# Attention and a feed-forward layer on one core: the two score groups of a head pair computed together, and a written order of the feed-forward products around them

## The chip, the core and the metric

One core of a Trainium2 chip. The metric is the device time of one execution in microseconds (us); lower is better. The core has TensorE (PE; its weight loads are listed as PEld), VectorE (DVE), ScalarE (ACT), GpSimd (POOL) and SyncE (SP), which issues nearly all transfers. Each engine works its own queue in order; semaphores join them.

## What is computed

Attention over 8 batches x 8 heads, head size 64, 512 local and 32 global tokens. A global query attends to all 544 keys; a local query to the 32 global keys and to the local keys within 32 positions. Then a feed-forward layer over the 4608 tokens:

```python
s_ll = np.where(np.abs(pos[:, None] - pos[None, :]) <= 32, scale * q_l @ k_l.T, -1e9)
out_l = sm(concat(scale * q_l @ k_g.T, s_ll)) @ concat(v_g, v_l)
out_g = sm(scale * q_g @ concat(k_g, k_l).T) @ concat(v_g, v_l)
x = attention output as (4608, 512)
h = x @ w_in                                   # 512 -> 2048
g = maximum(h, 0) + log1p(exp(-abs(h)))
out = g @ w_out                                # 2048 -> 512
```

Everything is in fp32. The feed-forward splits each operand in a high and a low part and forms three products (high x high, low x high, high x low).

## The kernel before

**Feed-forward** (`moe_items`). The tokens are worked in blocks: eight of 512 local tokens, b = 0 to 7 (one batch each), and one of 256 global tokens. A block has 16 tiles f of the hidden layer. The product H f (`hpart`) is 12 matmuls of 128x512 into one PSUM bank of the pool `ps_h` (tag `h`, two banks, used in turn). `act` follows: Abs, Exp and Ln on ACT, `e` on DVE (it reads the bank a last time), the high part `gh` on ACT, the low part `gl` on POOL. The product O f (`opart`, in two halves of two token tiles) is 12 matmuls from `gh`, `gl` and `w_out` into four banks that hold the block's output until O 15; then the results are copied out (`ot`, two on DVE and two on ACT). O f stands two H tiles behind H f. Before H 0 of a block, `split_x` makes `xh` (ACT) and `xl` (DVE) of the block's four inputs `xa`, one for each head pair of the batch.

**Attention.** The 32 head pairs m are four to a batch. Pairs 0 to 5 are worked ahead of the feed-forward, pairs 6 to 31 in pieces between its products. The pieces of a pair:
- `scores(m, 0)` and `scores(m, 1)`: each is 512 columns for both heads (chunks of 160, 192, 160 and of 32, 192, 192, 96), fp32, with 64 rows of the array to a head; into a two-bank tile of `ps_a` (tag `a`, one buffer, shared with the values). From pair 8 on DVE adds the mask while it reads the banks (L318) and takes the maxima of blocks (L319). Each group is followed by transfers of the next pair's queries and keys (`load`).
- `maxima` and `probs`: POOL and DVE fold the maxima (L331 to L344), DVE spreads them (L352), POOL subtracts (L355, five instructions), ACT takes the exponential (L357, one for each group), DVE sums blocks (L361).
- `totals`: the sums are folded and inverted (L331 to L372, result `rb`).
- `values` and `normalise`: 12 matmuls into the tile `a` (1024 columns for each head: chunks of 160, four times 192, and 96), then five DVE instructions (L392 to L397) that write `xa`.

The matmuls of scores and values are plain fp32, and each shows twice in the trace: 12 and 16 records for the two score groups, 24 for the values.

**Order.** Every piece has a slot number: 12 for each pair, plus 0 and 6 for the scores, 17 (`TOT`) for the totals and 21 (`VAL`) for the values. The feed-forward items are emitted in turn; after each, all pieces with a slot up to `at` are emitted, where `at` grows by 48 over a block. So a block holds four pairs, and the two score groups and the values of a pair stand at three places. The weights are split on ACT, DVE and POOL (L466 to L484) during block 0. A scheduling layer then places the instructions in the queues.

Of the kernel before, what the change touches and what calls it, by code (L numbers as in the profile page):

```python
# [8 lines left out]
F32 = mybir.dt.float32  # L9
# [4 lines left out]
ALU = mybir.AluOpType  # L14
# [5 lines left out]
P = 128  # L20
# [3 lines left out]
NPC = 3  # L24
# [8 lines left out]
MPE = 8  # L33
VAL = 21
TOT = 17
STEP = 3
GW = 75
W_AHEAD = 13
W_PRE = 16
START = 79  # L40
RATE = 3
# [15 lines left out]
def moe_over_global_local_attention(  # L57
# [235 lines left out]
    def scores(m, g):  # L293
        if "o" not in banks:
            ps = ps_s.tile([P, 2, 512], F32, tag=("oA", "oB")[g], name=f"s_ps{m}_{g}")
        else:
            ps = ps_a.tile([P, 2, 512], F32, tag="a", name=f"s_ps{m}_{g}")
        pe_mask = m < MPE
        cut = slice(512 * g, 512 * g + 512)
        for h in range(2 if pe_mask else 0):  # L300
            mm(ps[:, h], lhsT=ident, rhs=mask[:, cut], start=True, stop=False, skip_group_check=True)
        for c, o, qs, w in CHUNKS:
            if not cut.start <= o < cut.stop:
                continue
            raw, ks, o = st["raw", m, c // 2], QW[c // 2] + 128 * (c % 2), o - cut.start
            for h in range(2):
                r = slice(64 * h, 64 * h + 64)
                mm(ps[:, h, o:o + w], lhsT=raw[r, ks:ks + P], rhs=raw[r, qs:qs + w],
                   start=not pe_mask, stop=True, skip_group_check=True)
# [5 lines left out]
        if pe_mask:  # L315
            nc.scalar.copy(s, ps)  # L316
        else:
            nc.vector.tensor_tensor(s, ps, mask[:, cut].unsqueeze(1).to_broadcast([P, 2, 512]), op=ALU.add)  # L318
        order["scores"] = nc.vector.tensor_reduce(windows(st["mt", m], 4 + 16 * g, 36, 2, 16), s.rearrange("p h (b k) -> p h b k", k=32),  # L319
                                axis=AX.X, op=ALU.max, apply_transpose=True).ins  # L320

    def grid(t, start, *dims):
# [78 lines left out]
    def pieces():  # L401
        def piece(*fs):
            def go():
                for f in fs:
                    f()
            return go
        ps = []
        for m in range(M0, M):
            for g in range(2):
                fs = [lambda m=m, g=g: scores(m, g)]  # L410
                if m + 1 < M:
                    fs += [lambda m=m, p=p: load(m + 1, p) for p in ((0,), (1, 2))[g]]
                ps.append((12 * m + 6 * g, piece(*fs)))
                if g:
                    fs = [lambda m=m: maxima(m)] + [lambda m=m, q=q: probs(m, q) for q in range(2)]
                    ps.append((12 * m + (6 if m > M0 else 9), piece(*fs)))
            ps.append((12 * m + TOT, lambda m=m: totals(m)))
            fs = [lambda m=m: values(m), lambda m=m: normalise(m)]
            if m + 2 < M:
                fs.append(lambda m=m: load_v(m + 2))  # L420
            ps.append((12 * m + VAL, piece(*fs)))
        ps.sort(key=lambda t: t[0])
        return ps
# [74 lines left out]
    def moe_items():  # L498
# [119 lines left out]
    loads(W_PRE + 1)  # L618
    first = 12 * (H // 2 - 1) + VAL + STEP
    pcs = pieces()  # L620
# [12 lines left out]
    for k in range(-2, n + 2):  # L633
        stage(k + 2, 0)

        while k >= n - 2 and pcs[0][0] < min(12 * M0 + 4 * (k - n + 3), START):
            pcs.pop(0)[1]()
# [98 lines left out]
```

## Time and profile before

| | us |
|---|---|
| median of 3 runs (997.62 to 998.42) | 998.16 |
| the profiled execution | 998.89 |
| its span, first to last instruction | 997.0 |
| PE busy | 961.7 (96%), 5236 matmul records |
| PEld busy | 764.6 (77%) |
| DVE / ACT / POOL busy | 630.2 / 512.2 / 435.1 |

The profiled execution lies 1.9 us above its span, and 0.7 us above the median. On the page's chain that ended last PE holds 77%, of which the H and O products are 34% and 32% of the span, the scores 4% and the values 4%. A matmul's end is modelled and matmuls overlap in the records, so the distance from start to start tells more than the busy time.

### The profile page before, as it was taken

Reading aid. Unit: us, or ns where it says so; the run is one execution under the profiler, and the core shown is the slowest. Engines: PE = TensorE matmul, PEld = TensorE weight load, DVE = VectorE, ACT = ScalarE, POOL = GpSimd, SP = SyncE. Lnnn points to the kernel's source line nnn. Section 1 sums busy time; section 2 is a strip of 40 time slices with the busy share of each in tenths; the row PEclk is TensorE's granted clock in tenths of the full one; section 3 lists DMA queues with packets and bytes.
Section 4 is the critical chain, followed back from the end, with each engine's and each line's share of the span. In section 5 each row is a group of like instructions: output and inputs, shape, how many; then the busy total and the mean of one; then the engine's idle time right before and its main releaser. Section 6 shows DMA issues by size and latency. Waiting matters only on the chain.

```text
span 997.0 us, 14310 instructions
## 1 busy us (share of the span) xinstructions
PE 961.7 (96%) x5236; PEld 764.6 (77%) x5239; DVE 630.2 (63%) x1272; ACT 512.2 (51%) x890; POOL 435.1 (44%) x580
## 2 busy tenths in 40 slices
PE   6798999989999999999999999999999999999998
PEld 4576777767777777777787777777787788888896
DVE  6888959666668766776668666776677665311211
ACT  5785655644445544444455444454455445544553
POOL 5655756534444544443444444444434444222221
PEclk9897999989999999999999999999999999999999
DMA  9824231121112211121112111221112100200010
GB/s 363 304 76 160 96 99 35 59 74 40 37 49 70 70 49 39 47 91 33 49 50 80 39 49 49 70 70 38 48 48 75 49 17 2 65 1 1 1 43 22
DMA packets 34326, 66.20 MB, mean 66 GB/s; under 512 B 7632, under 2 KB 11472, under 8 KB 34256
## 3 DMA queue, kind: packets, MB, share of 16 engines
q1 hardware_dynamic: 33440, 65.19, 19.9%
q8 instruction: 41, 0.67, 0.3%
q14 instruction: 29, 0.24, 0.1%
q10 hardware_dynamic: 816, 0.10, 0.1%
HBM read 55.84 MB, written 9.44 MB: 65 GB/s over the span
## 4 chain that ended last, share of the span: by engine, by line
PE 77%; DVE 10%; POOL 5%; ACT 4%; issue 3%; POOLq 0%; ACTq 0%; DVEq 0%
PE h L124 34%; PE o L124 32%; PE s_ps L124 4%; PE v_ps L124 4%; POOL s L355 2%; POOL gl L533 1%; ACT e L171 1%; DVE mt L319 1%; DVE xl L439 1%; DVE wbitswi L475 1%; PE o0g L124 1%; DVE wiraw L478 1%; DVE woraw L478 1%; DVE sums L168 1%; DVE s L318 1%
## 5 line engine op out<-in xcount | busy, mean ns | idle before, releaser
L124 PE MATMUL h<-xh,wi 128*128 128x512 f32 (+1 forms) x1152 | 348.4, 386 | 6.0 <-DVE e L529 5.9
L124 PE MATMUL o<-wo,gh 128*128 128x512 f32 x1088 | 350.0, 403 | 3.0 <-ACT gh L532 3.0
L533 POOL TENSOR_TENSOR gl<-e,gh 128x512 fp32r<-128x512 f32 x136 | 180.3, 1326 | 314.1 <-ACT gh L532 281.9
L124 PEld LDWEIGHTS h<-xh,wi 128*128 128x128 f32 x1152 | 214.6, 191 | 54.1 <-DVE e L529 9.0
L529 DVE SCALAR_TENSOR_TENSOR e<-h,e 128x512 f32<-128x512 f32 x136 | 93.1, 685 | 248.1 <-ACT e L528 240.6
L124 PEld LDWEIGHTS o<-wo,gh 128*128 128x128 f32 x1088 | 199.0, 189 | 53.6 <-ACT gh L532 3.2
L124 PE MATMUL h<-xl,wi 128*128 128x512 f32 (+1 forms) x576 | 221.1, 384 | 0.0
L124 PE MATMUL o<-wo,gl 128*128 128x512 f32 x544 | 215.6, 396 | 2.3 <-POOL gl L533 2.3
L526 ACT ACTIVATE e<-h 128x512 f32<-128x512 f32 x136 | 81.0, 596 | 220.9 <-PE h L124 220.8
L355 POOL TENSOR_TENSOR s<-s,mb 128x320 f32<-128x320 f32 (+4 forms) x130 | 137.4, 1094 | 68.1 <-DVE mb L352 68.1
L532 ACT CAST gh<-e 128x512 fp32r<-128x512 f32 x136 | 84.5, 622 | 131.1 <-DVE e L529 131.1
L124 PEld LDWEIGHTS h<-xl,wi 128*128 128x128 f32 x576 | 109.7, 190 | 22.8
L124 PEld LDWEIGHTS o<-wo,gl 128*128 128x128 f32 x544 | 102.6, 189 | 29.3 <-POOL gl L533 5.5
L528 ACT ACTIVATE e<-e,one 128x512 f32<-128x512 f32 x136 | 98.8, 726 | 4.3
L527 ACT ACTIVATE e<-e 128x512 f32<-128x512 f32 x136 | 86.1, 633 | 3.8
L361 DVE TRANSPOSE_TENSOR_REDUCE zt<-s 128x32 f32<-128x1024 f32 x52 | 64.5, 1241 | 36.9 <-ACT s L357 36.9
L357 ACT ACTIVATE s<-s 128x1024 f32<-128x1024 f32 x52 | 55.1, 1059 | 31.9 <-POOL mt L312 28.4
L124 PEld LDWEIGHTS s_ps<-raw 64*128 64x128 f32 x728 | 53.9, 186 | 19.1 <-issue 19.1
L319 DVE TRANSPOSE_TENSOR_REDUCE mt<-s 128x32 f32<-128x1024 f32 x52 | 64.1, 1233 | 3.3 <-ACT s L316 2.7
L124 PE MATMUL s_ps<-raw 64*128 64x192 f32 (+3 forms) x728 | 64.4, 313 | 0.3
L318 DVE TENSOR_TENSOR s<-s_ps,mask 128x1024 f32<-128x1024 f32 x48 | 57.7, 1201 | 4.9 <-PE s_ps L124 4.9
L352 DVE STREAM_TRANSPOSE mb<-mt 128x512 f32<-128x512 f32 (+1 forms) x104 | 52.6, 565 | 0.8
(130 smaller groups left out, 826.0 us busy)
## 6 DMA issues: line engine op xcount, KB each, us to landing
raw<-in_qk SPq DMA_DIRECT2D x52, 272.0 KB, 2.7
v<-in_v SPq DMA_DIRECT2D x26, 384.0 KB, 3.1
out<-ot SPq DMA_DIRECT2D x34, 256.0 KB, 2.0
wiraw<-in_w_in SPq DMA_DIRECT2D x16, 512.0 KB, 9.0
woraw<-in_w_out SPq DMA_DIRECT2D x16, 512.0 KB, 8.5
raw<-in_qk SPq DMA_DIRECT2D x26, 224.0 KB, 2.8
v<-in_v SPq DMA_DIRECT2D x6, 512.0 KB, 6.1
raw<-in_qk SPq DMA_DIRECT2D x6, 416.0 KB, 7.9
```

Source lines behind the costliest of these rows:

```text
L124: order["pe"] = after(nc.tensor.matmul(*a, **k), "pe").ins
L318: nc.vector.tensor_tensor(s, ps, mask[:, cut].unsqueeze(1).to_broadcast([P, 2, 512]), op=ALU.add)
L319: order["scores"] = nc.vector.tensor_reduce(windows(st["mt", m], 4 + 16 * g, 36, 2, 16), s.rearrange("p h (b k) -> p h b k", k=32), axis=A ...
L355: nc.gpsimd.tensor_tensor(s[:, :, o:o + w], s[:, :, o:o + w], mb[:, :, q:q + w], op=ALU.subtract)
L357: nc.scalar.activation(s, s, AF.Exp, scale=0.125)
L361: nc.vector.tensor_reduce(windows(st["zt", m], 4 + 16 * g, 36, 2, 16), s.rearrange("p h (b k) -> p h b k", k=32), axis=AX.X, op=ALU.add, a ...
L526: nc.scalar.activation(e, ph, AF.Abs)
L527: nc.scalar.activation(e, e, AF.Exp, scale=-1.0)
L528: nc.scalar.activation(e, e, AF.Ln, bias=one)
L529: nc.vector.scalar_tensor_tensor(e, ph, 0.0, e, op0=ALU.max, op1=ALU.add)
L532: nc.scalar.copy(gh, e)
L533: nc.gpsimd.tensor_tensor(gl, e, gh.bitcast(F32), op=ALU.subtract)
```

## The change

Four things change.

1. From pair 9 on (`WIDE`) the two score groups are emitted together by `both_scores`. The first keeps the tile `a`; the second goes into two single banks of `ps_h`, those of the H products. DVE adds the mask of the second group in two instructions of 512 columns (one to a bank) in place of one of 1024. The three transfers of the next pair are emitted behind both groups, then the block maxima of both.
2. In blocks 1 to 6 the products follow the written list `ORDER`: H is a whole H tile, O a whole O tile, G the next pair's two score groups. Blocks 0, 7 and the global one keep their form.
3. The slots of pairs 6, 7 and 8 are written out (`SLOTS`); from pair 9 on maxima stand at 12 m + 5, totals at + 14, values at + 17.5. The start of block 1 is at slot 55.5 + 48 in place of 60 + 48.
4. Ahead of block 0, `START` is 76 in place of 79, and the slot grows by 3 a step in place of 4.

The core of the diff:

```diff
-VAL = 21
-TOT = 17
-STEP = 3
+VAL = 17.5
+TOT = 14
+WIDE = 9
+FIRST = 55.5
+SLOTS = {6: (72, 75, 78, 86, 90), 7: (81, 87, 87, 97.5, 101.5), 8: (92, 98, 98, 109, 113.5)}
+ORDER = "H O H H O G O H O H H O H O G O H O H H O H O G O H O H H O H H O G O O".split()
-START = 79
+START = 76
...
+        elif m >= WIDE and g:
+            ps = [ps_h.tile([P, 512], F32, tag="h", name=f"s_ps{m}_{g}_{h}") for h in range(2)]
         else:
             ps = ps_a.tile([P, 2, 512], F32, tag="a", name=f"s_ps{m}_{g}")
+        half = (lambda h: ps[h]) if isinstance(ps, list) else (lambda h: ps[:, h])
...
+        elif isinstance(ps, list):
+            for h in range(2):
+                nc.vector.tensor_tensor(s[:, h], ps[h], mask[:, cut], op=ALU.add)
...
+        if m < WIDE:
+            block_maxima(m, g)
...
+    def both_scores(m):
+        scores(m, 0)
+        scores(m, 1)
+        if m + 1 < M:
+            for p in range(NPC):
+                load(m + 1, p)
+        block_maxima(m, 0)
+        block_maxima(m, 1)
...
+            if 0 < b < B - 1:
+                if f == 0:
+                    h = iter(range(NF))
+                    for what in ORDER:
+                        if what == "H":
+                            f = next(h)
+                            items.append((b, 2, 0, lambda b=b, f=f: hpart(b, f, (0, 1))))
+                            items.append((b, 2, 0, lambda b=b, f=f: (hpart(b, f, (2, 3)), act(b, f))))
+                        elif what == "O":
+                            second(done, b)
+                            second(done + 1, b)
+                            done += 2
+                        else:
+                            m = next(wide, None)
+                            if m:
+                                items.append((b, 0, 0, lambda m=m: both_scores(m)))
+                continue
...
-        while k >= n - 2 and pcs[0][0] < min(12 * M0 + 4 * (k - n + 3), START):
+        while k >= n - 2 and pcs[0][0] < min(12 * M0 + 3 * (k - n + 3), START):
```

(`block_maxima` is the instruction of L319, moved into a function.) A block of the list reads, with the numbers of its tiles (O 15 of the block before stands behind H 0): H0 O15 H1 H2 O0 G O1 H3 O2 H4 H5 O3 H6 O4 G O5 H7 O6 H8 H9 O7 H10 O8 G O9 H11 O10 H12 H13 O11 H14 H15 O12 G O13 O14. The values of a pair are emitted behind H 3, H 7 and H 11 and behind O 13. Block 6 has only three G.

**Place 1: PE at the scores.** In the rows, `s_ps_0` is the first group, `s_ps_1` the second, `raw` the queries and keys, `o_0` the first output tile of an O product, `h` an H product. Before, inside block 3 (between the two pieces stand an O, an H, an O and an H product):

```order
L124 MATMUL h_12_4614<-xl_3_3926,wi_1463 128x512
L124 MATMUL s_ps_0_4636<-raw_0_4417 128x160 [waits DMAHW5_49,DVE_49,PE_49]
L124 MATMUL s_ps_0_4636<-raw_0_4417 128x160
L124 MATMUL s_ps_0_4636<-raw_0_4417 128x192 x2
L124 MATMUL s_ps_0_4636<-raw_1_4513 128x160 [waits DMAHW6_49]
L124 MATMUL s_ps_0_4636<-raw_1_4513 128x160
L124 MATMUL o_0_4079<-wo_1488,gh_10_4498 128x512 [waits Activation_49]
...
L124 MATMUL s_ps_1_4733<-raw_1_4513 128x32 [waits PE_49]
L124 MATMUL s_ps_1_4733<-raw_1_4513 128x32
L124 MATMUL s_ps_1_4733<-raw_1_4513 128x192 x2
```

After, at the last G of block 2:

```order
L127 MATMUL o_3_3078<-wo_1607,gl_12_3695 128x512
L127 MATMUL s_ps_0_3803<-raw_0_3571 128x160 [waits DMAHW5_49,PE_49]
L127 MATMUL s_ps_0_3803<-raw_0_3571 128x160
L127 MATMUL s_ps_0_3803<-raw_0_3571 128x192 x2
L127 MATMUL s_ps_0_3803<-raw_1_3573 128x160 [waits DMAHW6_49]
L127 MATMUL s_ps_0_3803<-raw_1_3573 128x160
L127 MATMUL s_ps_1_0_3814<-raw_1_3573 128x32 [waits DVE_49]
L127 MATMUL s_ps_1_1_3815<-raw_1_3573 128x32 [waits DVE_49]
L127 MATMUL s_ps_1_0_3814<-raw_1_3573 128x192
L127 MATMUL s_ps_1_1_3815<-raw_1_3573 128x192
L127 MATMUL s_ps_1_0_3814<-raw_2_3575 128x192 [waits DMAHW7_49]
L127 MATMUL s_ps_1_1_3815<-raw_2_3575 128x192
```

The second group follows the first with no product between, alternates between two tiles, and waits at its first two matmuls for DVE, which is the last reader of those banks.

**Place 2: ACT at the end of a block.** Here `e_14` and `e_15` are the last two tiles of block 3, `xh` the high parts of the next block's inputs. Before:

```order
L526 ACTIVATE e_14_4724<-h_14_4696 128x512 [waits PE_49,Pool_49]
L527 ACTIVATE e_14_4724<-e_14_4724 128x512 [waits Activation_49]
L528 ACTIVATE e_14_4724<-e_14_4724,one 128x512 [waits Activation_49]
L532 CAST gh_14_4729<-e_14_4724 128x512 [waits DVE_49]
L438 CAST xh_0_4871<-xa_0_4130 128x128 [waits PE_49]
L438 CAST xh_0_4871<-xa_0_4130 128x384
L438 CAST xh_1_4877<-xa_1_4361 128x128 [waits PE_49]
L438 CAST xh_1_4877<-xa_1_4361 128x384
L438 CAST xh_2_4883<-xa_2_4592 128x128 [waits PE_49]
L438 CAST xh_2_4883<-xa_2_4592 128x384
L526 ACTIVATE e_15_4801<-h_15_4788 128x512 [waits PE_49,Pool_49]
```

After:

```order
L548 ACTIVATE e_14_4717<-h_14_4704 128x512 [waits PE_49,Pool_49]
L460 CAST xh_0_4881<-xa_0_4160 128x128 [waits PE_49]
L460 CAST xh_0_4881<-xa_0_4160 128x384
L549 ACTIVATE e_14_4717<-e_14_4717 128x512 [waits Activation_49]
L460 CAST xh_1_4887<-xa_1_4393 128x128 [waits PE_49]
L460 CAST xh_1_4887<-xa_1_4393 128x384
L460 CAST xh_2_4893<-xa_2_4626 128x128 [waits PE_49]
L550 ACTIVATE e_14_4717<-e_14_4717,one 128x512 [waits Activation_49]
L460 CAST xh_2_4893<-xa_2_4626 128x384
L548 ACTIVATE e_15_4754<-h_15_4726 128x512 [waits PE_49,Pool_49]
L554 CAST gh_14_4722<-e_14_4717 128x512 [waits DVE_49]
L549 ACTIVATE e_15_4754<-e_15_4754 128x512 [waits Activation_49]
```

The six conversions of `xh` stood behind the work on tile 14; now they stand inside it, and the work on tile 15 begins behind them with `gh_14` between its first and second step.

**Place 3: ACT at the end of block 0.** `wbitswo` and `wo` belong to the last weight tile, `s_1638` to the scores of pair 8. Before:

```order
L532 CAST gh_14_1875<-e_14_1870 128x512 [waits DVE_49]
L357 ACTIVATE s_1638<-s_1638 128x2x512 [waits Pool_49]
L466 ACTIVATE wbitswo_1879<-woraw_1709 128x512 [waits DMAHW2_49]
L438 CAST xh_0_1983<-xa_0_902 128x512 [waits PE_49]
L438 CAST xh_1_1987<-xa_1_999 128x512 [waits PE_49]
L438 CAST xh_2_1991<-xa_2_1548 128x128 [waits PE_49]
L438 CAST xh_2_1991<-xa_2_1548 128x384
L357 ACTIVATE s_1638<-s_1638 128x2x512 [waits Pool_49]
L438 CAST xh_3_1997<-xa_3_1913 128x128 [waits DVE_49,PE_49]
L438 CAST xh_3_1997<-xa_3_1913 128x384 [waits DVE_49]
L526 ACTIVATE e_15_1936<-h_15_1923 128x512 [waits PE_49]
```

After:

```order
L460 CAST xh_0_1969<-xa_0_902 128x512 [waits PE_49]
L554 CAST gh_14_1875<-e_14_1870 128x512 [waits DVE_49]
L460 CAST xh_1_1973<-xa_1_999 128x512 [waits PE_49]
L380 ACTIVATE s_1638<-s_1638 128x2x512 [waits Pool_49]
L488 ACTIVATE wbitswo_1879<-woraw_1709 128x512 [waits DMAHW2_49]
L460 CAST xh_2_1977<-xa_2_1560 128x128 [waits PE_49]
L460 CAST xh_2_1977<-xa_2_1560 128x384
L548 ACTIVATE e_15_1913<-h_15_1900 128x512 [waits PE_49]
L380 ACTIVATE s_1638<-s_1638 128x2x512 [waits Pool_49]
L549 ACTIVATE e_15_1913<-e_15_1913 128x512 [waits Activation_49]
L460 CAST xh_3_1983<-xa_3_1935 128x128 [waits DVE_49]
L550 ACTIVATE e_15_1913<-e_15_1913,one 128x512 [waits Activation_49]
```

Here `xh_0` moves ahead of `gh_14`, `e_15` moves ahead of the second exponential, and the two conversions of `xh_3` end up among the steps of `e_15`. On PE the values of pair 7 stand behind H 15 in place of O 12, and the scores of pair 9 leave this place.

More of the change, by code (lines that the diff above doesn't have):

```diff
@@ L300, in scores @@
         for h in range(2 if pe_mask else 0):
-            mm(ps[:, h], lhsT=ident, rhs=mask[:, cut], start=True, stop=False, skip_group_check=True)
+            mm(half(h), lhsT=ident, rhs=mask[:, cut], start=True, stop=False, skip_group_check=True)
         for c, o, qs, w in CHUNKS:
@@ L307, in scores @@
                 r = slice(64 * h, 64 * h + 64)
-                mm(ps[:, h, o:o + w], lhsT=raw[r, ks:ks + P], rhs=raw[r, qs:qs + w],
+                mm(half(h)[:, o:o + w], lhsT=raw[r, ks:ks + P], rhs=raw[r, qs:qs + w],
                    start=not pe_mask, stop=True, skip_group_check=True)
@@ L316, in scores, with block_maxima @@
             nc.scalar.copy(s, ps)
+        elif isinstance(ps, list):
+            for h in range(2):
+                nc.vector.tensor_tensor(s[:, h], ps[h], mask[:, cut], op=ALU.add)
         else:
             nc.vector.tensor_tensor(s, ps, mask[:, cut].unsqueeze(1).to_broadcast([P, 2, 512]), op=ALU.add)
+        if m < WIDE:
+            block_maxima(m, g)
+    def block_maxima(m, g):
+        s = st["s", m][:, :, 512 * g:512 * g + 512]
         order["scores"] = nc.vector.tensor_reduce(windows(st["mt", m], 4 + 16 * g, 36, 2, 16), s.rearrange("p h (b k) -> p h b k", k=32),
                                 axis=AX.X, op=ALU.max, apply_transpose=True).ins
+    def both_scores(m):
[6 more added lines that the diff above has]
+        block_maxima(m, 1)
     def grid(t, start, *dims):
@@ L408, in pieces @@
         for m in range(M0, M):
-            for g in range(2):
+            g0, g1, mx, tot, val = SLOTS.get(m, (None, None, 12 * m + 5, 12 * m + TOT, 12 * m + VAL))
+            for g, slot in ((0, g0), (1, g1)) if m in SLOTS else ():
                 fs = [lambda m=m, g=g: scores(m, g)]
@@ L412, in pieces @@
                     fs += [lambda m=m, p=p: load(m + 1, p) for p in ((0,), (1, 2))[g]]
[L413 to L417, printed above, removed]
+                ps.append((slot, piece(*fs)))
+            ps.append((mx, piece(lambda m=m: maxima(m), *[lambda m=m, q=q: probs(m, q) for q in range(2)])))
+            ps.append((tot, lambda m=m: totals(m)))
             fs = [lambda m=m: values(m), lambda m=m: normalise(m)]
@@ L420, in pieces @@
                 fs.append(lambda m=m: load_v(m + 2))
-            ps.append((12 * m + VAL, piece(*fs)))
+            ps.append((val, piece(*fs)))
         ps.sort(key=lambda t: t[0])
@@ L568, in moe_items @@
         done = 0
+        wide = iter(range(WIDE, M))
         for i, (b, f) in enumerate(tiles):
@@ L571, in moe_items @@
                 items.append((b, 0, 0, lambda b=b: [split_x(b, j) for j in range(4)]))
+            if 0 < b < B - 1:
[15 more added lines that the diff above has]
+                continue
+            if f == 0 and b > 0:
                 second(done, b)
@@ L618, in moe_over_global_local_attention @@
     loads(W_PRE + 1)
-    first = 12 * (H // 2 - 1) + VAL + STEP
+    first = FIRST
     pcs = pieces()
```

## The prediction

> **What bounds the kernel now.** I read the span and the clock, the sums by stretch, the waits of PE and of its weight loads, and then single places of the timeline.
>
> ```profile
> core 0: 997.0 us, clock 0.984
> ...
> 100.00:200.00 100.00, 94.82 (x454) 74.54 (x456) 79.15 (x129) 61.52 (x100) 60.39 (x58) 0.97 0.23 72
> 500.00:600.00 100.00, 99.78 (x536) 78.78 (x536) 69.69 (x149) 48.32 (x76) 45.64 (x64) 1.00 0.18 54
> ...
> PE o L124 <- POOL gl L533: 1.1, 5, 0.2
> ...
> PEld s_ps L124 <- issue: 16.3, 45, 0.4
> PEld v_ps L124 <- issue: 8.7, 24, 0.4
> PEld o L124 <- POOL gl L533: 3.2, 5, 0.6
> ```
>
> In a stretch of blocks 1 to 6 (second row) PE is busy 99.78 of 100 us at clock 1.00, DVE 70, ACT 48, POOL 46. From 210 us on (the four wait rows) PE itself waits for another engine five times, 1.1 us together: nothing else is late there. So time can come only from PE's own stream, or from the ragged part before 210 us (first row: 94.82 busy, clock 0.97). PE's stream has one thing in it that is not products: at every start of scores or values the weight loads stand idle for up to 0.4 us, with no engine to blame.
>
> **The breaks in PE's stream, the first term.** Rows of PE's timeline (start, duration):
>
> ```profile
> 505.06 0.39 PE L124 MATMUL h<-xl,wi 128*128 128x512 f32 x1
> 505.38 1.14 PE L124 MATMUL s_ps<-raw 64*128 64x160 f32 x12
> ...
> 507.02 0.39 PE L124 MATMUL o<-wo,gl 128*128 128x512 f32 x1
> ...
> 511.88 0.39 PE L124 MATMUL h<-xl,wi 128*128 128x512 f32 x1
> 512.12 0.63 PE L124 MATMUL o<-wo,gh 128*128 128x512 f32 x2
> 512.58 0.39 PE L124 MATMUL o<-wo,gl 128*128 128x512 f32 x1
> ...
> 517.45 0.40 PE L124 MATMUL h<-xl,wi 128*128 128x512 f32 x1
> 517.77 1.34 PE L124 MATMUL s_ps<-raw 64*128 64x32 f32 x16
> ...
> 519.61 0.39 PE L124 MATMUL o<-wo,gl 128*128 128x512 f32 x1
> ...
> 524.47 0.40 PE L124 MATMUL h<-xl,wi 128*128 128x512 f32 x1
> 524.80 1.96 PE L124 MATMUL v_ps<-s,v 128*64 128x160 f32 x24
> ...
> 527.25 0.40 PE L124 MATMUL o<-wo,gl 128*128 128x512 f32 x1
> ```
>
> From the last matmul of an H product to the third of the next O takes 0.70 us with nothing between (511.88 to 512.58). With the first score group between it is 1.96 (505.06 to 507.02), so that group costs 1.26; the second costs 2.16 - 0.70 = 1.46; both 2.72. The values, as many columns for a head as both groups together (1024) but in one run, cost 2.78 - 0.70 = 2.08. So splitting 1024 columns costs up to 0.64. The scores have two chunks more (14 against 12 for each head), for which some 0.2 is left: joined I expect 2.3, 0.4 saved a pair. Bounds: 0.64 above; below, the edges alone, an entry of 0.32 in place of 0.24 (505.06 to 505.38, 511.88 to 512.12), and as much again at the exit, 0.2. There are 23 such pairs (9 to 31): **-9.2 us (-14.7 to -4.6).**
>
> **The waits that the change adds.** The second group needs both `h` banks, so it waits until DVE has read out the last two H tiles. Behind a single H tile (second and third G) that is met: H end, then these rows.
>
> ```profile
> L528 ACT ACTIVATE e<-e,one 128x512 f32<-128x512 f32 x136 | 98.8, 726 | 4.3
> L529 DVE SCALAR_TENSOR_TENSOR e<-h,e 128x512 f32<-128x512 f32 x136 | 93.1, 685 | 248.1 <-ACT e L528 240.6
> ...
> L526 ACT ACTIVATE e<-h 128x512 f32<-128x512 f32 x136 | 81.0, 596 | 220.9 <-PE h L124 220.8
> ...
> L532 ACT CAST gh<-e 128x512 fp32r<-128x512 f32 x136 | 84.5, 622 | 131.1 <-DVE e L529 131.1
> ...
> L527 ACT ACTIVATE e<-e 128x512 f32<-128x512 f32 x136 | 86.1, 633 | 3.8
> ...
> L318 DVE TENSOR_TENSOR s<-s_ps,mask 128x1024 f32<-128x1024 f32 x48 | 57.7, 1201 | 4.9 <-PE s_ps L124 4.9
> ...
> 192.18 0.65 DVE L529 SCALAR_TENSOR_TENSOR e<-h,e 128x512 f32<-128x512 f32 x1
> ...
> 192.86 0.62 ACT L532 CAST gh<-e 128x512 fp32r<-128x512 f32 x1 [4.87 <-DVE e L529]
> ...
> 522.60 2.10 ACT L438 CAST xh<-xa 128x128 fp32r<-128x128 f32 x6 [1.19 <-PE h L124]
> ```
>
> 0.60 + 0.63 + 0.73 + 0.69 is 2.65; hand-overs take 0.03 each or a little more (`e` ends at 192.83, `gh` starts at 192.86), 0.25 with a margin: 2.9 behind the end of H; the second group starts at 2.8 (an O product, 12 x 0.233 by the rows above) + 0.9 (first group) = 3.7. That leaves 0.8. The same banks must be free again for the H product behind G O: the mask of group one (1.20), its maxima (1.23, of the same size) and the first half mask (0.69, as L529, which reads 512 columns too) end 4.3 behind the start of G, the H product starts at 5.1. The two half masks cost DVE 0.17 more than one L318, 23 times; DVE has 30% free there. The loads of the next pair move behind both groups on SP's queue, ahead of that pair's transfer of `v`; the next G is at least 23 us away, so they cost nothing unless a transfer took that long.
>
> *Last G of blocks 1 to 5 (place 2).* Behind the end of H 14 ACT does Abs (0.60), the six conversions (2.10), Exp and Ln of tile 14, then Abs 15, `gh_14`, Exp and Ln 15: 0.60 + 2.10 + 1.36 + 0.60 + 0.62 + 1.36 = 6.65, with hand-overs 6.9; DVE's `e_15` ends at 7.6. PE, with H 15, O 12 and the first group, is there at 2.8 + 2.8 + 0.9 = 6.5. A wait of 1.0 (0 if the scheduler's order is kinder than my walk, 2.0 if `e_13` is late too), 5 times: **+5.0 (0 to +10).**
>
> *First G of a block.* The chain starts at the last G of the block before:
>
> ```profile
> 494.93 1.25 DVE L319 TRANSPOSE_TENSOR_REDUCE mt<-s 128x32 f32<-128x1024 f32 x1
> 498.81 2.03 DVE L352 STREAM_TRANSPOSE mb<-mt 128x512 f32<-128x512 f32 x4
> 499.67 5.21 POOL L355 TENSOR_TENSOR s<-s,mb 128x320 f32<-128x320 f32 x5 [2.56 <-DVE mb L352]
> 502.44 1.06 ACT L357 ACTIVATE s<-s 128x1024 f32<-128x1024 f32 x1
> 504.91 1.06 ACT L357 ACTIVATE s<-s 128x1024 f32<-128x1024 f32 x1 [1.42 <-POOL mt L312]
> ```
>
> Counted from that G's start, DVE is at `e_15` until 2.0, then mask 1.2, maxima 1.2, half masks 1.4: the last maxima begin at 5.8. L352 follows 3.9 later (494.93 to 498.81), plus some 2.3 for the normalising and `xl` steps queued between (an estimate: seven instructions of 0.2 to 0.5, as this trace has them); POOL 0.9 behind it, at 12.9; the exponentials 2.8 and 5.2 later, the second from 18.1 to 19.2. Then ACT's queue holds `gh_0`, two output copies (0.6 each, sized as Abs), Abs to Ln of tile 1, and Abs, Exp, `gh_1`, Ln of tile 2: 0.6 + 1.2 + 2.0 + 2.6, to 25.6, and `e_2` ends at 26.3. PE (seven products of 2.8, values 1.9, both groups 2.3, the wait of 1.0, and 0.9 of the next G) wants the bank at 25.7. A wait of 0.5 to 0.6, 5 times (block 1 has no such G ahead): **+2.5 (0 to +10).** It has no margin on either side, so the upper bound is wide.
>
> The five waits for `gl` go, since no G stands ahead of an O that follows its own H closely: between 1.1 (PE's wait) and 3.2 (its weight loads'), **-1.9.**
>
> **The end of block 0 (place 3).**
>
> ```profile
> 204.26 1.62 PE L124 MATMUL o<-wo,gh 128*128 128x512 f32 x2 [2.97 <-ACT gh L532]
> 206.31 0.79 PE L124 MATMUL o<-wo,gl 128*128 128x512 f32 x1 [0.43 <-POOL gl L533]
> ...
> 213.72 0.63 PE L124 MATMUL h<-xh,wi 128*128 128x512 f32 x2
> ...
> 193.35 0.63 PE L124 MATMUL o<-wo,gh 128*128 128x512 f32 x2
> ...
> 204.26:210.75 6.49, 6.02 (x13) 4.04 (x13) 6.30 (x11) 0.59 (x1) 2.11 (x3) 0.50 0.11 40
> ```
>
> From 193.35 to 213.72 PE does O 13, O 14, O 15, H 0 and one score group: 4 x 2.8 + 1.26 = 12.5 of work in 20.4 us. 7.9 are lost: waits for `gh_15`, which waited behind DVE's last weight and `xl` steps, and behind the wait a clock of 0.50. Afterwards tile 15's ACT steps stand earlier and its H 0 nearer. Walking the new queues with the durations above, O 14 waits 1.0 for `gl_14`, H 0 1.4 for the last `xl`, O 15 1.2 for `gl_15`: 3.6 lost, in three small pieces. **-4.3 (-7.9 to 0,** if those waits join into one long one). The moved slots of pairs 6 to 8 shift two pieces by one product each; the wait near 166 us stands behind the same DVE steps in another order: 0, within 2 either way.
>
> **The sum:** -9.2 + 5.0 + 2.5 - 1.9 - 4.3 = -7.9. From the profiled execution's 998.9 that is 991.0; the median of the runs lies 0.7 lower than that execution, so **990.3 us**, 0.8% less.
>
> **The rivals.**
>
> *Slower: the banks decide.* At the ten first and last G the wait is 2.1 us, not 1.0 and 0.5: ACT or DVE late by 1.1 to 1.6, the size of one more queued step and one exponential. Against 7.5 in the sum that is 21, so 1003.8. A gap of that size also costs clock:
>
> ```profile
> 168.70 0.73 PE L124 MATMUL h<-xh,wi 128*128 128x512 f32 x2 [2.12 <-DVE e L529]
> ...
> 168.70:173.60 4.90, 4.90 (x15) 3.90 (x15) 4.31 (x5) 3.48 (x6) 3.15 (x2) 0.65 0.00 0
> ```
>
> Behind a gap of 2.12 us the granted clock is 0.65 over 4.9 us, 1.7 us lost; ten times that, 1021. Break-even is 1.5 us a wait (15.4 over ten). For it speaks that both waits hang on ACT's strict order; against it that ACT is half idle. [...]
>
> *No change: the joint is small.* Joining saves only the edges (-4.6) and the end of block 0 keeps its loss: +4.6 + 4.3 on the sum, 999.2. For it speaks that each weight load of a score chunk has to be issued all the same; against it the values' single run.
>
> *Much faster: no wait at any G.* Then -7.5 more, 982.8. For it speaks that the scheduling layer placed instructions by when it saw them ready; against it the queues of place 2 as they stand.
>
> **Chances.** The sum as it stands, 986 to 996: 0.55. No waits: 0.17. No change: 0.10. Banks decide: 0.18. The range takes in the no-wait case with its bounds and the no-change case and leaves most of the slow one out: 981 to 1000. A change of 0.2% is about what the runs of this kernel (997.62 to 998.42) tell from none. Faster 0.72, same 0.10, slower 0.18.
>
> **What would show it.** Joined scores: one run of 28 records in about 2.0 us, 23 waits of `issue` at `s_ps` gone. Waits: PE or its loads for DVE's `e` at `s_ps`, about 1.0 at the last G and 0.5 at the first, none at the middle ones. End of block 0: no PE wait above 2 us, the clock there near 1. Wrong if `s_ps` waits for DVE at middle G too, if the clock falls inside blocks 1 to 6, or if H 3 waits for a half mask.

## The result and the profile after

The changed kernel takes **983.88 us** (median of 4 runs, 983.69 to 985.04) against 997.89 for the kernel before in the same session (997.29 to 998.42): a ratio of 0.9862, interval 0.9849 to 0.9874, or 14.0 us less. The forecast was 990.3, in a range of 981 to 1000. The sign and the range held. The gain is nearly twice the forecast: the time lies outside the 986 to 996 that had 0.55 of the chances, and beside the rival "no wait at any G" (982.8).

The profiled execution took 983.79 us, its span is 982.0 (997.0 before) and its mean granted clock 0.986 (0.984 before). Two stretches (us of PE, PEld, DVE, ACT and POOL busy, granted clock, DMA share), then all waits of PE and its weight loads from 210 us on (sum, times, longest):

```profile
100.00:200.00 100.00, 94.72 (x449) 74.60 (x452) 81.36 (x127) 60.41 (x97) 61.79 (x56) 0.95 0.22 72
500.00:600.00 100.00, 99.96 (x564) 80.84 (x563) 72.08 (x158) 47.25 (x78) 41.34 (x62) 1.00 0.18 55
...
PEld v_ps L127 <- issue: 8.7, 24, 0.4
PEld s_ps L127 <- issue: 6.5, 18, 0.4
PEld s_ps L127 <- PE o L127: 1.8, 5, 0.4
PEld s_ps L127 <- DVE e L551: 0.5, 3, 0.2
```

Scores have 23 gaps of up to 0.4 in place of 45 (18 under `issue`, and five that the view puts down to PE's own `o`), since a pair now has one entry into scores, not two. The values keep theirs (24). The five waits for `gl` are gone, and no row of PE itself is left: inside blocks 1 to 6 PE is busy 99.96 of 100 us. The stretch from 100 to 200 us is no better than before (94.72 busy against 94.82).

The joined run at the first G of block 4, and ahead of it in time the one at the last G of block 3, on PE's timeline (start, duration):

```profile
536.82 2.21 PE L127 MATMUL s_ps<-raw 64*128 64x160 f32 x28
538.95 0.73 PE L127 MATMUL o<-wo,gh 128*128 128x512 f32 x2
...
512.59 2.65 PE L127 MATMUL s_ps<-raw 64*128 64x160 f32 x28
515.17 0.73 PE L127 MATMUL o<-wo,gh 128*128 128x512 f32 x2
```

The 28 records take 2.13 us from their first start to the next product, at a first G as at a middle one. At the last G they take 2.58: 0.44 more, which no row calls a wait of PE (only the last wait row above, of the weight loads, shows three of the five). The two chains that the prediction walked, in DVE's and ACT's rows around those G:

```profile
513.16 0.69 DVE L551 SCALAR_TENSOR_TENSOR e<-h,e 128x512 f32<-128x512 f32 x1 [1.58 <-POOL gl L555]
513.78 1.23 DVE L327 TENSOR_TENSOR s<-s_ps,mask 128x1024 f32<-128x1024 f32 x1
...
517.49 1.25 DVE L333 TRANSPOSE_TENSOR_REDUCE mt<-s 128x32 f32<-128x1024 f32 x1
...
523.10 2.02 DVE L375 STREAM_TRANSPOSE mb<-mt 128x512 f32<-128x512 f32 x4
...
536.69 0.69 DVE L551 SCALAR_TENSOR_TENSOR e<-h,e 128x512 f32<-128x512 f32 x1
...
510.22 0.50 ACT L460 CAST xh<-xa 128x384 fp32r<-128x384 f32 x1
510.62 0.59 ACT L548 ACTIVATE e<-h 128x512 f32<-128x512 f32 x1
511.15 0.62 ACT L554 CAST gh<-e 128x512 fp32r<-128x512 f32 x1
511.67 0.63 ACT L549 ACTIVATE e<-e 128x512 f32<-128x512 f32 x1
512.34 0.72 ACT L550 ACTIVATE e<-e,one 128x512 f32<-128x512 f32 x1
```

At the last G `e_15` ends at 513.85, and the second group could have started at 512.59 + 0.97 = 513.56: late by 0.3 and a hand-over. At the first G that follows, `e_2` ends at 537.38 and the second group is due at 536.82 + 0.97 = 537.79: met, with 0.41 to spare.

**Where the 15.0 us of the two spans come from.** Read at two marks, the start of H 14 of block 0 (182.94 before, 185.18 after) and the point where O 0 of block 1 and the scores of pair 9 that stand by it are done (223.44, 218.29): up to the first mark 2.2 lost; between the marks 40.5 became 33.1, 7.4 won; behind the second 773.6 became 763.7, 9.9 won.

### The profile page after: what moved, and what is told of

The parts are those of the page before. It is cut to its first block, busy times and chain, and to the rows that moved or that the text cites. A ratio compares the mean times of both kernels' runs of the same rounds, so it can differ in the third digit from the quotient of the medians.

```text
span 982.0 us, 14339 instructions
## 1 busy us (share of the span) xinstructions
PE 946.7 (96%) x5236; PEld 763.9 (78%) x5239; DVE 638.3 (65%) x1295; ACT 502.8 (51%) x890; POOL 434.4 (44%) x580
## 4 chain that ended last, share of the span: by engine, by line
PE 84%; DVE 9%; ACT 3%; issue 1%; POOL 1%; POOLq 0%; ACTq 0%; DVEq 0%
PE o L127 37%; PE h L127 36%; PE s_ps L127 5%; PE v_ps L127 5%; DVE wbitswi L497 1%; ACT e L174 1%; DVE wiraw L500 1%; DVE wbitswo L497 1%; DVE sums L171 1%; PE s L127 1%; DVE woraw L500 1%; DVE wbitswi L495 1%; DVE wbitswo L495 1%; PE s0g L127 0%; DVE zt L393 0%
## 5 line engine op out<-in xcount | busy, mean ns | idle before, releaser
L127 PE MATMUL o<-wo,gh 128*128 128x512 f32 x1088 | 345.6, 399 | 0.0
L127 PEld LDWEIGHTS o<-wo,gl 128*128 128x128 f32 x544 | 102.3, 188 | 24.8 <-POOL gl L555 1.0
L354 POOL COPY mt<-mt 32x75 f32<-32x75 f32 x78 | 19.0, 244 | 94.5 <-DVE mt L333 92.4
L127 PE MATMUL s_ps<-raw 64*128 64x192 f32 (+3 forms) x728 | 60.2, 308 | 0.5
L375 DVE STREAM_TRANSPOSE mb<-mt 128x512 f32<-128x512 f32 (+1 forms) x104 | 52.6, 562 | 0.7
```

The source lines that it names most:

```text
L127: order["pe"] = after(nc.tensor.matmul(*a, **k), "pe").ins
L375: nc.vector.transpose(mb[:, :, o:o + 32 * n].rearrange("p h (s k) -> p h s k", k=32), windows(e, k, 21, 2, n).unsqueeze(3).to_broadcast([P ...
```

## The experiments

Each is the changed kernel with one thing altered; none leaves work out. All but one were timed against the kernel before (997.7 to 998.2 in these sessions).

**1. The joint undone** (the joint: the two groups of a pair in one run). The second group is a run of its own, in the tile `a`, behind the O product after G, and the last G of a block stands one O product earlier:

```diff
-        elif m >= WIDE and g:
+        elif False:
...
+                            if m:
+                                items.append((b, 0, 0, lambda m=m: second_scores(m)))
```

> The changed kernel with the joint undone: from pair 9 on the second group is a run of its own, behind the O product that follows G, in the same two activation-free banks as the first group; each group's maxima stand behind its mask again. The list of products is the changed kernel's, except that the last G of a block stands one O earlier (H H G O O O), so that the second group and the values don't meet. Theory (the joint is worth 0.45 us a pair, the rest of the gain is the order): 983.9 + 23 x 0.45 - 5 x 0.44 (the second group needs no h bank, so the wait at the last G goes) = 992.1 us; each group again has a weight-load gap of its own at s_ps, PE waits for nothing from 220 us on. Rival 1 (the list of products alone brings the gain, joining nothing): 981.7 us. Rival 2 (the joint is worth 0.64, the upper bound of the prediction): 996.4 us.

Measured: 995.64 us, ratio 0.9976 (0.9967 to 0.9984), 11.8 above the changed kernel. The first G of block 4, to be held beside the rows above, and below it a wait of PE:

```profile
540.64 0.61 PE L127 MATMUL o<-wo,gh 128*128 128x512 f32 x2
...
543.45 1.14 PE L127 MATMUL s_ps<-raw 64*128 64x160 f32 x12
...
547.52 1.34 PE L127 MATMUL s_ps<-raw 64*128 64x32 f32 x16
...
551.76 0.49 PE L127 MATMUL v_ps<-s,v 128*64 128x160 f32 x4
...
PE h L127 <- DVE xl L462: 2.6, 5, 0.5
```

O, first group, O, second group, H take 11.12 (540.64 to 551.76); the same work joined takes 10.71 in the changed kernel (534.00 to 544.71). **The joint is worth 0.41 us.** The last row is a wait that this edit brought: at the first H of a block the last `xl` is late; from start to start that H takes 3.54, not 2.75, five times, 4.0 together. From the first G to the end the kernel is 11.2 longer; less the 4.0, plus the 2.2 that the last G no longer loses, 9.4 are left, and 9.4 / 23 is 0.41 again. So the size is near that of the theory (0.45), which had not seen the `xl` wait and came out 3.5 too low in time. The rival without a joint is out; 0.64 a pair comes closer in time (996.4), but the distance at the place itself excludes it.

**2. The same price on the values.** Each pair's values in two runs with half an O product between them:

```diff
-        for k, o, c, w in VALUES:
+        for k, o, c, w in VALUES[3 * half:3 * half + 3]:
...
+            ps.append((val, lambda m=m: values(m, 0)))
+            fs = [lambda m=m: values(m, 1), lambda m=m: normalise(m)]
...
-            ps.append((val, piece(*fs)))
+            ps.append((val + 0.8, piece(*fs)))
```

> The changed kernel with the values of every pair in two runs of 6 records instead of one of 12 (24 records in two columns of the array), half an O product between them; the normalising waits for the second half. Scores stay joined. Theory (what the joint saved is the price of one more switch between products and other runs, the same for any such run): pairs 8 to 31 pay 0.47 each, 983.9 + 24 x 0.47 = 995.2 us. Rival 1 (the price belongs to the scores, whose first matmuls wait for something of their own): under 0.15 each, at most 987.5 us. Rival 2 (the edges alone, 0.2 each, the lower bound of the prediction): 988.7 us.

Measured: 1000.00 us, 1.0019 (1.0011 to 1.0028), 16.1 above the changed kernel.

```profile
PEld v_ps L127 <- issue: 17.4, 48, 0.4
PEld h L127 <- DVE xl L464: 8.1, 5, 1.6
...
525.65 1.14 PE L127 MATMUL v_ps<-s,v 128*64 128x160 f32 x12
526.72 0.73 PE L127 MATMUL o<-wo,gh 128*128 128x512 f32 x2
...
528.31 1.04 PE L127 MATMUL v_ps<-s,v 128*64 128x192 f32 x12
```

The gaps of issue at the values doubled, to 48. Of the time, 8.1 is again the `xl` wait at block starts (the last half of the values, and with it `normalise` and `xl`, came later); the rest is 8.0, or 0.33 for each of 24 extra switches. O, values, O with the split take 8.12 from start to start, without it 7.79: 0.33. The first rival (a price of the scores alone) is out: one more switch costs time at the values too. The theory had the same price for both, 0.47, and 995.2 us; it is 0.41 for scores and 0.33 for values, and the theory had not seen the `xl` wait. In both experiments a piece delayed at the end of a block reaches PE through the next block's `xl`.

**3. The list decides whether the banks are free.** H and O alternate, each G straight behind an H:

```diff
-ORDER = "H O H H O G O H O H H O H O G O H O H H O H O G O H O H H O H H O G O O".split()
+ORDER = "H O H H O H G O H O H O H O H G O H O H O H O H G O H O H O H O H G O O".split()
```

> The changed kernel with another list of products for blocks 1 to 6: H and O alternate and every G stands straight behind an H product. Then the bank that the second group needs last is that of the H product just ended. Theory (the places in the list, not spare room on DVE, keep the joint free of waits): the chain Abs, Exp, Ln, e takes 2.9 us from H's end, the first group covers 0.9 of it, so each of the 23 G waits 2.0 us; 983.9 + 46 = 930 is excluded, the time is 983.9 + 46 = 1029.9 us, or, if each wait also lowers the clock as behind the 2.12 us gap of the kernel before (1.7 us each), 1069. Rival (the banks come free early enough anyway, the scheduling would have gone well with any list): within 5 us of 983.9.

(The "930 is excluded" in this text is a slip; its theory is 1029.9, or 1069 with the clock.) Measured, one run with the profile: 1064.55 us. The waits, two of them on the timeline, and the stretches around those two:

```profile
PE s_ps L127 <- DVE e L551: 41.5, 23, 1.9
...
343.70 1.33 PE L127 MATMUL s_ps<-raw 64*128 64x32 f32 x14 [1.79 <-DVE e L551]
...
522.84 2.08 PE L127 MATMUL s_ps<-raw 64*128 64x32 f32 x14 [1.79 <-DVE e L551]
...
340.63:349.63 9.00, 7.21 (x63) 6.04 (x64) 6.65 (x12) 2.57 (x4) 2.00 (x4) 1.00 0.31 90
519.78:528.78 9.00, 7.21 (x43) 5.93 (x44) 6.15 (x10) 2.57 (x4) 1.98 (x4) 0.81 0.34 91
```

All 23 G wait: the rows call it 1.8 each, where the chain Abs, Exp, Ln, `e` behind an H product had been added up to 2.0. From the start of a G to the next product it is 4.32 us where the clock stays (340.63 to 344.96), so a wait costs 2.18 against the 2.14 of the changed kernel. The last two rows are the 9 us from the start of two such G. At one the granted clock stays at 1.00; at the other it is 0.81, 1.7 us lost (0.19 of 9), behind a gap of the same 1.79 us. Of the 23 G 18 show 0.81 and five 1.00. Together that is 23 x 2.18 - 5 x 0.44 (which the last G lost already) + 18 x 1.7 = 78.5 of the 80.7 us. So the rival "the banks decide" describes a real mechanism with nearly the price given to it; the list keeps the kernel out of it by placing an O product ahead of every G.

**4. and 5. The last G later.** First by one product, then by half of one (`o` is half an O product):

```diff
-ORDER = "... H O H H O G O O".split()
+ORDER = "... H O H H O O G O".split()        # 4
+ORDER = "... H O H H O o G o O".split()      # 5
```

with the probabilities of that pair moved by the same distance, and in the first the values of the pair before ahead of that G.

> The changed kernel with the last G of blocks 1 to 5 one product later (H H O O G O in place of H H O G O O), the values there one product earlier, ahead of that G, and the probabilities of the pair 1.2 products later. Theory (the 0.44 us at the last G are a wait for the e of tile 15, which is then met): 983.9 - 5 x 0.44 = 981.7 us, all 23 joined runs within 2.2 us. Rival 1 (the place later makes the chain behind it late: maxima, probabilities, and with them e_2 ahead of the next first G): the wait moves to the first G of blocks 2 to 6, and the time is 983.9 or above, up to 988. Rival 2 (the 0.44 us are not a wait but the first read of a bank just written): 983.9 us and the same longer runs.

> The changed kernel with the last G of blocks 1 to 5 half a product later: H H O o G o O, where o is half an O product (6 matmuls, 1.4 us); the probabilities of that pair stand half a product later too. Theory (the 0.44 us there are a wait for e of tile 15, and the place one whole product later failed only because one O product and nothing else was left ahead of the next H): the second group finds its banks free with 0.9 to spare, behind G stand 1.4 + 2.1 (values) + 2.8 before the next H, more than the half masks need: 983.9 - 5 x 0.44 = 981.7 us, no wait row for a half mask. Rival 1 (the half masks still come late, since e of tile 15 is ahead of them on DVE): h waits for a half mask at 5 places, 984 to 990 us. Rival 2 (breaking the O product costs about 0.2 at the extra switch): 982.7 us.

Measured: 996.06 (0.9982, 0.9971 to 0.9992) and 988.99 (0.9909, 0.9896 to 0.9923): 12.2 and 5.1 above the changed kernel. The waits of PE from 210 us on, of the first and then of the second, each with what stands ahead of one such wait on the timeline:

```profile
PE h L127 <- DVE s L325: 9.2, 5, 1.8
...
543.83 2.51 POOL L555 TENSOR_TENSOR gl<-e,gh 128x512 fp32r<-128x512 f32 x2 [0.95 <-PE o L127]
...
544.46 0.67 DVE L361 COPY zt<-zt 32x6 f32<-32x6 f32 x1
545.16 1.22 DVE L389 TENSOR_SCALAR zt<-zt 32x42 f32<-32x42 f32 x1
546.30 1.20 DVE L327 TENSOR_TENSOR s<-s_ps,mask 128x1024 f32<-128x1024 f32 x1
...
550.26 0.84 PE L127 MATMUL h<-xh,wi 128*128 128x512 f32 x2 [1.84 <-DVE s L325]
```

```profile
PE s_ps L127 <- DVE e L551: 5.3, 5, 1.1
...
537.77 1.61 DVE L393 COPY zt<-zt 32x21 f32<-32x21 f32 x3
...
537.88 1.28 POOL L555 TENSOR_TENSOR gl<-e,gh 128x512 fp32r<-128x512 f32 x1 [2.35 <-ACT gh L554]
```

In both the 0.44 at the last G are gone (2.14 and 2.13 there), so it was a wait for `e_15`. In both the loss is at the **first G of the next block**. Ahead of that G DVE's queue holds the folds of the last G's pair (`zt`); they stand later now.

In experiment 4 they meet the masks: the mask of the first group starts 2.1 behind the end of its matmuls (546.30, where they end at 544.2), the half masks after it, and H 3 waits 1.84 for a bank, 9.2 in five blocks. Behind three of the five the clock falls too (0.72 over 550.00 to 556.00; of the stretches of 100 us from 300 to 800, which hold one of the five each, the first, third and fifth have 0.98, the second and fourth 1.00). In experiment 5 `e_2` is late and the second group itself waits, 1.48 from start to start.

In both, the folds are not only later but longer. L361 and L389 take 0.67 and 1.22 in experiment 4, and L393 takes 1.61 in experiment 5, where the changed kernel has 0.15, 0.18 and 0.54 at this place: they now run beside a `gl` on POOL, and the last of them ends 0.04 behind its end in the one (546.38, 546.34) and 0.22 behind it in the other (539.38, 539.16). The added length is 1.56 of the 2.1 by which the mask is late and 1.07 of the 1.33 by which `e_2` is late (it ends at 540.83, the second group is due at 539.50; estimates from these rows; DVE has no gap in between), and the five waits are alike: 9.2 for five of at most 1.8, and 5.3 for five of at most 1.1.

So the rival of experiment 4 had the place right (the first G), but not the form (a half mask, not `e_2`) nor the price, which I had put at 4 at most; in experiment 5 the time of rival 1 came (984 to 990), but by luck: its wait, a half mask at the place moved, did not. Both theories had 981.7 and are out. No run moves the last G later and keeps these folds clear of POOL, so what the move alone would cost is not shown.

**6. The chain itself shortened.** At the boundaries into blocks 2 to 6 the last of ACT's six conversions stands behind Ln of tile 15:

```diff
-            nc.scalar.copy(hi, f(t))
+            i = nc.scalar.copy(hi, f(t))
+            if 1 < b < B - 1 and j == 2 and o:
+                after(i, "ln")
```

> The changed kernel with one conversion held back: at the boundaries into blocks 2 to 6 the last of ACT's six conversions that are due there (xh of the third quarter, 128x384, 0.50 us) is ordered behind Ln of tile 15, and by the order built for this gh of tile 14 now stands behind Exp of tile 15 too; on DVE the xl made from that conversion stands between e of tile 15 and the mask of the first group. Nothing else moves. Theory (the 0.44 us at the last G of blocks 1 to 5 are ACT's queue ahead of e of tile 15, which has 0.5 to 1.0 too much in it): e ends 0.5 to 1.0 earlier, the wait goes, the mask starts no later: 983.9 - 5 x 0.44 = 981.7 us, all 23 joined runs 2.13 long. Rival 1 (DVE's queue is the tight one: the xl ahead of the mask makes the chain to the next first G late, where the slack is 0.4): the wait reappears at the first G of blocks 2 to 6, 983 to 987 us. Rival 2 (gh of tile 14 comes later and O 14 waits for its gl): 983 to 985 us, with a wait row for gl.

Measured: 981.88 us (980.97 to 983.26), 0.9840 (0.9826 to 0.9853).

```profile
513.31 2.21 PE L127 MATMUL s_ps<-raw 64*128 64x160 f32 x28
515.45 0.73 PE L127 MATMUL o<-wo,gh 128*128 128x512 f32 x2
...
513.42 0.69 DVE L553 SCALAR_TENSOR_TENSOR e<-h,e 128x512 f32<-128x512 f32 x1 [1.59 <-ACT e L552]
...
514.50 1.22 DVE L327 TENSOR_TENSOR s<-s_ps,mask 128x1024 f32<-128x1024 f32 x1
```

The same last G takes 2.14 now, `e_15` starts 0.11 behind the start of the scores where it had started 0.57 behind, the mask 1.19 behind, as before the edit. From the first G of block 1 to the end this kernel is 2.1 shorter (763.8 against 765.9; the theory had 2.2). The two medians differ by as much, 2.0, but their intervals overlap, so the proof is the trace. So the cause is ACT's queue ahead of `e_15`, and the cure is less work in it, not a later place: at the next first G all runs still take 2.14 or 2.15, no wait.

**7. The end of block 0: O 15 ahead of H 0 again**, in block 1 alone:

```diff
-                    for what in ORDER:
+                    for what in ("O H H H O G".split() + ORDER[6:] if b == 1 else ORDER):
```

> The changed kernel with one thing undone at the end of block 0: O 15 of block 0 stands ahead of H 0 of block 1 (O H H H O G), as in the kernel before, not behind it; nothing else moves. Theory (block 0's end is paced by DVE, whose e of tile 15 ends 202.5 us into the span whatever PE does; the 7.3 us that the end got shorter came from H 0, which now runs while gh and gl of tile 15 are made): O 15 stands ready at 201.2 and waits 1.9 for gh and about as long again for gl, 3.3 more than now, so 987.2 us, and 988.9 if the clock falls behind it. Rival (the end got shorter because pair 9's first group no longer stands there, which stays so here): 983.9 us.

Measured: 988.69 us, 0.9904 (0.9891 to 0.9918), 4.8 above the changed kernel; the theory with the clock had 988.9. Its waits there and the clock behind them, and below them the same places of the changed kernel:

```profile
202.78 0.50 PE L127 MATMUL o<-wo,gh 128*128 128x512 f32 x1 [2.85 <-ACT gh L554]
...
204.98 0.77 PE L127 MATMUL o<-wo,gl 128*128 128x512 f32 x1 [0.73 <-POOL gl L555]
...
203.00:209.00 6.00, 4.80 (x13) 3.38 (x13) 4.88 (x12) 0.59 (x1) 2.03 (x3) 0.72 0.12 44
```

```profile
205.39 0.50 PE L127 MATMUL o<-wo,gl 128*128 128x512 f32 x1 [0.73 <-POOL gl L555]
...
204.26:210.75 6.49, 5.76 (x25) 4.48 (x25) 4.64 (x9) 3.49 (x6) 2.48 (x3) 1.00 0.23 84
```

The wait of 2.97 for `gh_15` of the kernel before is back (2.85), and behind it a lowered clock, 0.72 over 6.0 us (1.7 lost; 0.50 over 6.49 in the kernel before, 3.2 lost). The theory had 1.9 for `gh` and 1.9 for `gl`; the sum is about right, the split is not. Pair 9's scores stayed where the change put them, so the rival is out: the greater part of what the end of block 0 gained, 4.8 of 7, clock included, is that H 0 runs while `gh` and `gl` of tile 15 are made.

**8. to 10. The moved slots.** The positions of pairs 6 to 8 as before, then those of pair 6 alone, then pair 6 together with experiment 6:

```diff
-SLOTS = {6: (72, 75, 78, 86, 90), 7: (81, 87, 87, 97.5, 101.5), 8: (92, 98, 98, 109, 113.5)}
+SLOTS = {6: (72, 75, 77.897, 85.483, 89.276), 7: (80.741, ...), 8: (92.121, ...)}   # 8
+SLOTS = {6: (72, 75, 77.897, 85.483, 89.276), 7: (81, 87, ...), 8: (92, 98, ...)}   # 9 and 10
```

> The changed kernel with the positions of pairs 6 to 8 put back to where the kernel before has them (72, 75, 77.9, ... as fractions of the new scale; the joint, the list and everything from pair 9 on as changed; one side effect: the values of pair 8 in block 1 stand ahead of H 3 and not behind it). Theory A (the wait near 166 us, +2.4, and the shorter end of block 0, -7.3 with one joint of 0.45 in it, both come from these positions): 983.9 - 2.4 + 6.9 = 988.4 us. Theory B (the wait comes from these positions, the end of block 0 got shorter because pair 9's scores moved out of it, behind O 0 of block 1): 981.5 us. Theory C (both come from elsewhere, the positions are worth nothing): 983.9 us.

> The changed kernel with the positions of pair 6 alone as in the kernel before (its values stand ahead of O 6 of block 0, not behind it). Theory (from 165 to 202 us DVE has more queued than it can do, so PE's waits there only change places): the wait near 166 us shrinks from 3.2 to 2.1, PE runs ahead by some 3 us, and loses it again at the end of block 0, where it waits for gl of tile 14: 983.9 us, within 1. Rival (the two stretches are independent): 983.9 - 3.3 = 980.6 us.

> The same conversion held back, and the positions of pair 6 as in the kernel before. Theory (the first is worth 2.2, the second nothing, since DVE paces that stretch): 981.7 us, equal to the one without the second. Rival (the 0.5 us by which the kernel with pair 6 alone lay lower is real): 981.2 us.

Measured: 985.16 (0.9874, 0.9860 to 0.9889), 983.40 (0.9855, 0.9840 to 0.9870) and 981.07 (0.9833, 0.9819 to 0.9846). Neither of the first two differs from the changed kernel (0.9849 to 0.9874) beyond the intervals: theory C of the first. The theory of the second had the time right and the way wrong: its wait near 166 us is still 3.4, not 2.1, and it does not wait for the `gl` of tile 14. PE's waits in this stretch, of the changed kernel, then of the one with all old positions:

```profile
169.63 1.22 PE L127 MATMUL h<-xh,wi 128*128 128x512 f32 x2 [3.23 <-DVE e L551]
```

```profile
168.52 0.74 PE L127 MATMUL h<-xh,wi 128*128 128x512 f32 x2 [2.12 <-DVE e L551]
...
197.47 0.50 PE L127 MATMUL o<-wo,gl 128*128 128x512 f32 x1 [1.74 <-POOL gl L555]
```

With the old positions PE reaches H 13 3.4 us sooner (174.76 against 178.12), and gives it all back ahead of block 1: H 0 starts at 200.8 there and at 201.2 in the changed kernel. Over the profiles of all kernels here with H 0 ahead of O 15, H 13 starts anywhere from 172.9 to 178.1 and H 0 between 199.5 and 201.7, and the earliest H 13 has the latest H 0 (experiment 2). So it is not PE that sets the start of block 1. At the end of the stretch DVE is full, in the middle it is not, as two rows of the changed kernel show (DVE's is the third busy time):

```profile
180.00:185.00 5.00, 5.00 (x33) 3.97 (x32) 2.17 (x3) 3.15 (x6) 1.55 (x3) 1.00 0.61 167
...
195.00:200.00 5.00, 5.00 (x29) 4.01 (x26) 5.00 (x9) 3.21 (x6) 2.67 (x4) 1.00 0.24 79
```

That DVE's work at the end of block 0 sets the pace is the likely reading; no run makes that work shorter, so it is argued and not shown. What is shown is that time won near 166 us is lost again by H 0. The tenth kernel, the conversion and pair 6 together, is the fastest of the study: 2.8 us below the changed kernel, with an interval that just clears it. It cannot be told from experiment 6 (0.9826 to 0.9853), so neither its theory nor its rival is decided.

## Why the prediction was right, and where it was off

| term of the sum | forecast | measured |
|---|---|---|
| joined scores, 23 | -9.2 | -9.4 |
| last G of blocks 1 to 5 | +5.0 | +2.2 |
| first G of a block | +2.5 | 0 |
| five `gl` waits go | -1.9 | -3.0 (a remainder; -2.4 at the places themselves) |
| end of block 0 | -4.3 | -7.0 |
| moved slots, wait near 166 us | 0 within 2 | +2.2 |
| sum | -7.9 | -15.0 |

- **The joint** was right in kind and size: 0.4 forecast, 0.41 measured by its removal, one run of 28 records in 2.13 (forecast about 2.0) with one entry. It came from the rows of the values, which are one run of 1024 columns; and a switch of its own on the values costs 0.33.
- **Last G**: the mechanism was right (`e_15` late, waited for there and nowhere else), the size was off: 0.44 instead of 1.0. The failed step is the walk of ACT's queue, which added mean durations end to end, 7.6 from H 14's end to the end of `e_15`; the trace has 7.0, since the records of instructions that do not depend on each other overlap there: Abs 15 (0.59) starts 0.40 behind a conversion of 0.50, `gh` (0.62) 0.53 behind Abs, Exp 0.52 behind `gh`, 0.06 to 0.10 less than the one ahead of each lasts. Ln 15, which reads what Exp 15 writes, starts 0.04 behind its end.
- **First G**: no wait, a slack of 0.41 where the walk had 0.5 to 0.6 of wait. Counted from the last G's start `e_2` ends at 24.8 (forecast 26.3) and the bank is wanted at 25.2 (25.7). The walk was 0.9 late at the last maxima (4.9, not 5.8) and another 0.6 at L375 (10.5, not 12.0), where it had taken 2.3 for the normalising steps. That this place "has no margin on either side" was right: in experiment 5 the first G starts 22.39 behind the last one, 24.23 in the changed kernel, and that made five waits (with the longer folds described there).
- **`gl` waits**: 9.87 won behind the second mark, less 22 joints of 0.41, plus 2.2, leave 3.0; that is a remainder, and other small waits of the weight loads went too (`o` for ACT's `e`, 2.7; `h` for DVE's `e`, 1.7). At the five places the half O product takes 1.98 from start to start (533.55 to 535.53 in the kernel before), where the other halves behind a score group take 1.50: 0.48 each, 2.4 together. That lies between PE's own row (1.1) and the weight loads' (3.2), as the forecast did.
- **End of block 0 and the slots**: 7.4 won between the marks, 0.4 of it one joint; 2.2 lost ahead. The clock there is 1.00 in place of 0.50, as forecast. Of the three small waits that the walk found, O 15's came (0.73 in its row, 1.1 from start to start; forecast 1.2), H 0's did not, and O 14's came or not by when PE got there: none in the profiled execution, 1.5 and 1.6 in experiments 4 and 6, which have the same order at that place and reach H 14 at 182.7 and 182.3, not 185.2. Behind the wait near 166 us the clock is 0.50 in the profiled execution and 1.00 in those two, so the missing wait at O 14 is luck. Against the kernel before, H 12 starts 0.9 later (the wait there is 3.23, not 2.12), and the H and O products behind it take 1.3 longer at the lower clock; together 2.2, just beyond the forecast's 2. Experiment 8 shows that the two terms are one: what is lost at the first is won at the second. Their sum, -4.8, lies near the forecast -4.3. Which of the moved slots lengthened the first wait is open (not pair 6 alone, by experiment 9), and no run takes `FIRST`, `START` and the slower growth of the slot apart from them.

So the sum was off by 7, of which 5.3 are waits at G that were priced too high and 1.1 the remainder beside the `gl` waits. None of the three signs of being wrong came: no wait at a middle G, no fall of the clock inside blocks 1 to 6, no H 3 waiting for a half mask. The rival "no wait at any G" had the better size (982.8); its reason, that the instructions stand as the scheduling layer saw them ready, is not shown: at the last G the order was as walked, and it was the durations that overlapped. That the time came out by this rival owes as much to the end of block 0 and the remainder as to G: the waits at G still cost 2.2.

## What to carry to other kernels

A switch between runs of different shape on TensorE had a price here (0.41 and 0.33 us) that shows only as a gap of up to 0.4 ahead of the weight loads (in the changed kernel 42 of 47 under `issue`): read it from start to start, at the place where one run is already whole, and count the switches. A wait that was removed by moving a piece later was paid at the next place of the same chain; look for the slack there first, and for what the moved work will run beside, and shorten the chain if there is none. And before a wait of PE is priced, look whether the stretch that it stands in starts the next one later at all: near 166 us up to 3.4 us of PE's time were worth nothing at the end.

## What the runs showed of the hardware

- **The clock fell behind gaps of 1.8 to 3.2 us, and not each time.** In experiment 3, in one execution, 18 of the 23 gaps of 1.8 to 1.9 us were followed by 0.81 over 9 us (1.7 us lost each), five by 1.00. The mean clocks agree: 0.958 over a span of 1062.8 there and 0.986 over 982.0 in the changed kernel are 44.6 and 13.7 us lost, a difference of 30.9, where 18 x 1.7 is 30.6. In experiment 4 the three shortest of twelve executions (993.55 to 993.90) have a mean clock of 0.987, the other nine (995.58 to 998.83) 0.978 to 0.982. Near 166 us a gap of 3.2 us was followed by 0.50 over 5 us in the changed kernel, and one of 3.4 us by 1.00 in experiment 4:

```profile
170.00:175.00 5.00, 5.00 (x13) 3.85 (x13) 4.31 (x4) 3.71 (x7) 3.72 (x3) 0.50 0.00 0
```

```profile
170.00:175.00 5.00, 4.99 (x21) 3.98 (x22) 4.29 (x4) 3.68 (x8) 3.55 (x3) 1.00 0.00 0
```

What makes the clock fall behind one such gap and not behind another, no run here shows.

- **Some tiny DVE instructions took longer beside a POOL instruction, others did not.** COPY steps (L361, L393) and TENSOR_SCALAR (L389) on at most 32x42 elements take 0.15 to 0.18 each in the changed kernel, with POOL idle beside them (534.40 to 535.78). In the rows of experiment 4 L361 starts at 544.46 and L389 at 545.16, while POOL makes two `gl` from 543.83 to 546.34, and they take 0.67 and 1.22: L361 ends at 545.13, where the first `gl` is done at about 545.1 (an estimate, half of the two), L389 at 546.38. The reductions L358 and L360 (TENSOR_REDUCE), at 544.06 and 544.21 beside the same first `gl`, take their usual 0.22. In the changed kernel none of these steps is stretched ahead of the first G (L393 is through at 535.78, POOL's `gl` starts at 536.17); experiments 4 and 5 lose that.
